# Output projection loaded in two transfers of 16 rows to a partition, last copy split over two engines, biases loaded from the ACT queue

## Chip, cores, metric

One core of one Trainium2 chip. The metric is the device time of one execution in microseconds (us), lower is better. The profiler's span (134.7 us for the kernel before) starts at the first instruction and is about 2 us shorter than the device time. Of the core's engines, PE is TensorE (matmuls), DVE is VectorE, ACT is ScalarE, Pool is GpSimd and SP is SyncE, which here only issues loads. A slice row of a profile cuts the span into 40 parts: a digit is the busy share in tenths, PEclk the clock granted to PE in tenths of full speed.

## The reference, cut to what matters

One decode step of a layer with attention and an MLP in parallel: batch 2, one token, model width 576. Attention has 32 query heads on 16 K/V heads of width 128, over the last 2048 positions of the caches.

```python
# _A_ref: q = xn @ wq; softmax over the last W = 2048 cached positions
scores = jnp.einsum("bhqd,bhkd->bhqk", q, k) * (Dh ** -0.5)
p = _softmax(scores, axis=-1)
o = jnp.einsum("bhqk,bhkd->bhqd", p, v)
return (...o.transpose(0, 2, 1, 3)...).reshape(B, Sq, Hq * Dh) @ wo     # wo: 4096 x 576
# _B_ref: relu(xn @ w1 + b1) ** 2 @ w2 + b2, w1: 576 x 4608
return x + _A_ref(xn, ...) + _B_ref(xn, ...)
```

With two rows of activations everything is a matter of reading 53.6 MB once: K and V (33.6 MB), wq, wo, w1, w2.

## The kernel before

All large loads go through SP's DMA queue, in program order. K and V come in units of four K/V heads of one batch item (eight units, 2 MB of K and 2 MB of V each). PE transposes K, ACT and DVE move K^T from PSUM to SBUF, PE forms scores, and after the softmax PE forms P·V. The results of two units (one group of 8 query heads, both batch items) go through `wo_sel`, which sorts head dimensions into the row order of the wo tile, and `wo_acc`, which multiplies by wo into the accumulator `out_ps`. The MLP's products go into the same accumulator.

```python
def issue_wo(tq):                               # WR = 8 rows of wo to a partition: 9216 contiguous bytes
    tl = wopool.tile([P, WR, D], BF16, tag="wo_sb", name=f"wo_{tq}")      # wopool: 2 buffers
    n = NC * Dh
    nc.sync.dma_start(out=tl[:], in_=A_wo[tq * n:(tq + 1) * n, :].rearrange("(p r) n -> p r n", r=WR))
# ... cut ...
def out_acc(lhsT, rhs_of, start=False, stop=False):      # two matmuls of 288 columns
    for i in range(2):
        nc.tensor.matmul(out_ps[32 * i:32 * i + B, :], lhsT=lhsT, rhs=rhs_of(i * OH, (i + 1) * OH), ...)
# ... cut: order of issue ...
load_k(1); load_v(0); load_k(2); load_v(1); issue_wo(0); load_k(3)
# ... issue_wo(1) after load_k(4); issue_wo(2), issue_wo(3) after the last V; then w2 in six pieces
for u in (NU - 2, NU - 1):
    for g in range(NG):
        pv(u, g)
wo_acc(NQ - 2)
mlp_x()                      # w2x: the rows of w2 that five small ACT-queue loads bring, 26 matmuls
wo_sel(NQ - 1)
wo_acc(NQ - 1)
for i in range(len(W2P)):    # the six w2 pieces, 68 matmuls
    mlp_o(*W2P[i], last=(i == len(W2P) - 1))
nc.vector.tensor_copy(out=fin_sb[:], in_=out_ps[:])      # 34 partitions x 288, fp32 to bf16
nc.sync.dma_start(out=out2d[:, 0:OH], in_=fin_sb[0:B, :])
nc.scalar.dma_start(out=out2d[:, OH:D], in_=fin_sb[32:32 + B, :])
```

## Time and profile before

| | before |
|---|---|
| device time, first three runs | 136.68 us (136.67 to 136.73) |
| span of the profiled run | 134.7 us |
| SP's queue | 53.32 MB in 4612 packets, 94.3% of the 16 engines' time |
| PE busy | 75% |
| last byte of w2 landed (packet records) | 131.13 us |

The third line is the one to read: a share of 16 DMA engines near its ceiling means that the time is a sum of packets. "Packet records" means the single DMA packets of the trace, with start, duration and size; the trace does not tell on which engine each ran. The lines of the views stand in the prediction.

### The profile page before, as it was taken

How to read it: one execution, taken by the hardware profiler on the slowest of the kernel's cores; microseconds unless marked ns; L12 is line 12 of the kernel's file. 1: busy time of each engine (PE TensorE's matmuls, PEld its weight loads, DVE VectorE, ACT ScalarE, POOL GpSimd, SP SyncE). 2: the span in 40 equal slices, each digit the busy share in tenths (PEclk: the TensorE clock that was granted, in tenths of full speed). 3: DMA queues.
4: the chain of work that ended last, by engine and by line, in shares of the span. 5: the costliest groups of instructions: out<-in, count | busy, mean ns of one | idle time of the engine just before them, and what ended most of it. 6: DMA issues, size and time to landing. Idle time of an engine off the chain costs nothing.

```text
span 134.7 us, 4124 instructions
## 1 busy us (share of the span) xinstructions
PE 100.8 (75%) x1876; PEld 83.2 (62%) x1876; DVE 56.9 (42%) x135; ACT 44.3 (33%) x51; POOL 9.7 (7%) x31
## 2 busy tenths in 40 slices
PE   1036797639999677998796998797194997599961
PEld 0025374639999665996786997784034997544630
DVE  7522045552277366346555655645105246500001
ACT  6706033470537207335534635421012451100000
POOL 7300000110010011001101001001100001100000
PEclk9999999555558965589996899997555579755797
DMA  4999999999999999999999999999999999999960
GB/s 152 409 422 434 428 433 419 438 414 439 404 418 439 415 412 433 410 426 429 423 428 419 423 421 422 430 415 423 408 442 428 428 424 407 416 413 424 398 235 1
DMA packets 4772, 53.87 MB, mean 400 GB/s; under 512 B 614, under 2 KB 764, under 8 KB 1280
## 3 DMA queue, kind: packets, MB, share of 16 engines
q1 hardware_dynamic: 4612, 53.32, 94.3%
q8 instruction: 14, 0.23, 0.7%
q10 hardware_dynamic: 80, 0.30, 0.5%
q0 software_dynamic: 64, 0.01, 0.0%
q14 instruction: 2, 0.02, 0.0%
HBM read 53.62 MB, written 0.00 MB: 398 GB/s over the span
## 4 chain that ended last, share of the span: by engine, by line
DMA 87%; PE 8%; SPq 2%; issue 0%; DVE 0%; ACT 0%; ACTq 0%
DMA v<-in_A_v_cache_dram 47%; DMA k<-in_A_k_cache_dram 18%; DMA w<-in_B_w_dram 16%; PE kT_ps L279 5%; DMA w2x_sb<-in_B_w_dram 5%; PE oT_ps L331 1%; PE sc_ps L294 1%; SPq L110 1%; SPq L117 1%; PE out_ps L244 1%; SPq L122 0%; DVE fin_sb L505 0%; ACT kT L282 0%; ACTq L282 0%
## 5 line engine op out<-in xcount | busy, mean ns | idle before, releaser
L279 PE MATMUL kT_ps<-ident,k 128*128 128x128 bf16 x512 | 49.5, 265 | 3.8 <-DMA k<-in_A_k_cache_dram 2.6
L279 PEld LDWEIGHTS <-k 128*128 128x128 bf16 x512 | 40.4, 121 | 5.3 <-DMA k<-in_A_k_cache_dram 2.8
L282 ACT COPY kT<-kT_ps 128x1024 bf16<-128x1024 bf16 x32 | 31.9, 1011 | 34.5 <-PE kT_ps L279 33.1
L284 DVE COPY kT<-kT_ps 128x1024 bf16<-128x1024 bf16 x32 | 21.6, 683 | 26.6 <-PE kT_ps L279 26.1
L294 PE MATMUL sc_ps<-qT_all,kT 128*128 128x8 bf16 x512 | 21.8, 168 | 5.1 <-ACT kT L282 2.6
L294 PEld LDWEIGHTS <-kT 128*128 128x128 bf16 x512 | 19.7, 101 | 7.0 <-ACT kT L282 3.4
L331 PE MATMUL oT_ps<-pT,v 128*128 128x8 bf16 x512 | 15.9, 167 | 3.9 <-DMA v<-in_A_v_cache_dram 2.2
L331 PEld LDWEIGHTS <-v 128*128 128x128 bf16 x512 | 14.5, 97 | 5.3 <-issue 2.7
L311 ACT ACTIVATE pT<-sub 128x512 bf16<-128x512 f32 x8 | 5.0, 630 | 25.8 <-DVE sub L308 25.8
L313 DVE TENSOR_REDUCE l<-pT 128x8 f32<-128x512 bf16 x8 | 8.6, 1070 | 4.7 <-ACT pT L311 4.7
L304 POOL PARTITION_ALL_REDUCE gmax<-m x8 | 2.9, 365 | 80.6 <-DVE m L302 80.6
L244 PEld LDWEIGHTS <-hT_sb 128*2 128x2 bf16 (+2 forms) x94 | 4.8, 97 | 5.1 <-issue 2.3
L300 DVE TENSOR_REDUCE m<-sc_ps 128x8 f32<-128x512 f32 x8 | 5.5, 691 | 3.8 <-PE sc_ps L294 3.5
L374 PE MATMUL h_ps<-w,xnT 128*2 128x384 bf16 x48 | 4.2, 518 | 3.2 <-DMA w<-in_B_w_dram 3.2
L244 PE MATMUL out_ps<-wo,ws 128*2 128x288 bf16 x64 | 6.5, 363 | 0.0
L244 PE MATMUL out_ps<-w,hT_sb 128*2 128x288 bf16 x68 | 5.5, 306 | 1.1 <-DMA w<-in_B_w_dram 0.8
L505 DVE CAST fin_sb<-out_ps 34x288 bf16<-34x288 f32 x1 | 0.5, 450 | 13.4 <-PE out_ps L244 13.4
L308 DVE TENSOR_TENSOR sub<-sc_ps,gm 128x512 f32<-128x512 f32 x8 | 5.5, 690 | 0.2
L374 PEld LDWEIGHTS <-xnT 128*2 128x2 bf16 x60 | 1.8, 115 | 5.8 <-issue 5.8
L315 POOL PARTITION_ALL_REDUCE lsum<-l x8 | 3.2, 398 | 24.6 <-DVE l L313 24.6
L257 PE MATMUL q_ps<-wq,xnT 128*2 128x512 bf16 x32 | 3.3, 475 | 2.0 <-DMA wq<-in_A_wq_dram 2.0
L244 PE MATMUL out_ps<-b_sb,ones_b 1*2 1x288 bf16 x2 | 0.4, 394 | 5.5 <-DMA b_sb<-in_B_b_dram 5.5
(72 smaller groups left out, 47.7 us busy)
## 6 DMA issues: line engine op xcount, KB each, us to landing
k<-in_A_k_cache_dram SPq DMA_DIRECT2D x8, 2048.0 KB, 36.0
v<-in_A_v_cache_dram SPq DMA_DIRECT2D x8, 2048.0 KB, 27.7
wo<-in_A_wo_dram SPq DMA_DIRECT2D x4, 1152.0 KB, 24.1
w<-in_B_w_dram SPq DMA_DIRECT2D x2, 2304.0 KB
wq<-in_A_wq_dram SPq DMA_DIRECT2D x2, 2048.0 KB, 14.8
w<-in_B_w_dram SPq DMA_DIRECT2D x3, 1296.0 KB
w_rem<-in_B_w_dram SPq DMA_DIRECT2D x1, 576.0 KB
w<-in_B_w_dram SPq DMA_DIRECT2D x1, 576.0 KB, 26.2
```

Of the source, the lines that this page charges most:

```text
L244: nc.tensor.matmul(out_ps[32 * i:32 * i + B, :], lhsT=lhsT, rhs=rhs_of(i * OH, (i + 1) * OH), start=start, stop=stop, skip_group_check=True)
L257: nc.tensor.matmul(q_ps[k][32 * g:32 * g + B, :], lhsT=xnT[:, xc, :], rhs=rhs, start=(c == 0), stop=(c == KC - 1), skip_group_check=True, ...
L279: nc.tensor.transpose(out=kT_ps[:, i * P:(i + 1) * P], in_=k_sb[:, j * Dh:(j + 1) * Dh], identity=ident[:])
L282: nc.scalar.copy(out=kT[:], in_=kT_ps[:])
L284: nc.vector.tensor_copy(out=kT[:], in_=kT_ps[:])
L294: nc.tensor.matmul(sc_ps[:, g * JG + i, :], lhsT=kT[:, i * P:(i + 1) * P], rhs=qT_all[:, b, tq * NC:(tq + 1) * NC], start=True, stop=True)
L300: nc.vector.tensor_reduce(out=m1[:], in_=sc_ps[:].rearrange("p j c -> p c j"), axis=AX.X, op=ALU.max)
L308: nc.vector.tensor_tensor(out=sub[:], in0=sc_ps[:], in1=gm2[:].unsqueeze(1).to_broadcast([P, NJ, NC]), op=ALU.subtract)
L311: nc.scalar.activation(out=pT[:], in_=sub[:], func=ACT.Exp, scale=scale)
L313: nc.vector.tensor_reduce(out=l1[:], in_=pT[:].rearrange("p j c -> p c j"), axis=AX.X, op=ALU.add)
L331: nc.tensor.matmul(oT_ps[:], lhsT=v_sb[:, j * Dh:(j + 1) * Dh], rhs=pT_tiles[u][:, j, :], start=(j == 0), stop=(j == NJ - 1))
L374: nc.tensor.matmul(mlp["ps"][k][32 * g:32 * g + B, :], lhsT=xnT[:, xc, :], rhs=rhs, start=False, stop=(c == KC - 1), skip_group_check=True ...
```

## The change

Its intent: fewer, larger wo packets and half as many projections, each of twice the matmuls; a shorter last copy; less work on Pool.

```diff
-    WR = NC * Dh // P
+    WR = 2 * NC * Dh // P                    # 16 rows to a partition: 18432 bytes
-    wopool = ctx.enter_context(tc.tile_pool(name="wopool", bufs=2))
+    wopool = ctx.enter_context(tc.tile_pool(name="wopool", bufs=1))
+        n = P * WR                           # in issue_wo: two loads of 2304 KB
 ... selection matrix: one memset and one reduction in place of eight copies on Pool (cut) ...
 ... wo_sel: two head groups at once, 16 selection matmuls (cut) ...
-    issue_wo(0) ... issue_wo(1) ... issue_wo(2) ... issue_wo(3)
+        if u == 4:
+            issue_wo(0)                      # before w1
+    issue_wo(1)                              # before w2
-    nc.gpsimd.dma_start(out=b1_sb[:], ...)   # and b2
+    nc.scalar.dma_start(out=b1_sb[:], ...)
     step(NU - 1, {}, with_pv=False)
+    for g in range(NG):
+        pv(NU - 2, g)
+    mlp_x()                                  # its matmuls kept in program order
+    for g in range(NG):
+        pv(NU - 1, g)
+    wo_sel(1)
+    wo_acc(1)
-    nc.vector.tensor_copy(out=fin_sb[:], in_=out_ps[:])
+    nc.vector.tensor_copy(out=fin_sb[:, 0:half_o], in_=out_ps[:, 0:half_o])
+    nc.scalar.copy(out=fin_sb[:, half_o:OH], in_=out_ps[:, half_o:OH])
```

More of the change, by code (lines that the diff above doesn't have):

```diff
@@ L79 @@
     OH = D // 2
-    WR = NC * Dh // P
+    NP = NQ // 2
+    WR = 2 * NC * Dh // P
     DW = Dh // WR
@@ L136, in w_rows, with issue_wo @@
         return tiles[c][:, col0 - sg * L:col0 - sg * L + n], NFULL + sg
-    def issue_wo(tq):
-        tl = wopool.tile([P, WR, D], BF16, tag="wo_sb", name=f"wo_{tq}")
-        n = NC * Dh
-        nc.sync.dma_start(out=tl[:], in_=A_wo[tq * n:(tq + 1) * n, :].rearrange("(p r) n -> p r n", r=WR))
-        wo_tiles[tq] = tl
+    def issue_wo(t):
+        tl = wopool.tile([P, WR, D], BF16, tag="wo_sb", name=f"wo_{t}")
+        n = P * WR
+        nc.sync.dma_start(out=tl[:], in_=A_wo[t * n:(t + 1) * n, :].rearrange("(p r) n -> p r n", r=WR))
+        wo_tiles[t] = tl
     w2_last = []
@@ L229 @@
     rmask = const.tile([P, WR], BF16, name="rmask")
-    gsel = const.tile([P, DW], BF16, name="gsel")
-    sel = const.tile([P, NC, NC, DW], BF16, name="sel")
+    MZ = (2 * NC - 1) * DW
+    sel = const.tile([P, 2 * MZ + DW], BF16, name="sel")
     nc.gpsimd.memset(sel[:], 0.0)
@@ L234, with out_acc @@
         nc.vector.tensor_reduce(out=rmask[:], in_=ident[:].rearrange("p (c r) -> p r c", r=WR), axis=AX.X, op=ALU.add)
-        nc.vector.tensor_reduce(out=gsel[:], in_=ident[:].rearrange("p (c r) -> p c r", r=WR), axis=AX.X, op=ALU.add)
-    for h in range(NC):
-        nc.gpsimd.tensor_copy(out=sel[:, h, h, :], in_=gsel[:])
+        nc.vector.tensor_reduce(out=sel[:, MZ:MZ + DW], in_=ident[:].rearrange("p (c r) -> p c r", r=WR), axis=AX.X,
+                                op=ALU.add)
     out_ps = psum.tile([32 + B, OH], F32, tag="out", name="out_ps")
     nc.vector.memset(out_ps[:], 0.0)
-    def out_acc(lhsT, rhs_of, start=False, stop=False):
+    def out_acc(lhsT, rhs_of, start=False, stop=False, pin=False):
         for i in range(2):
-            nc.tensor.matmul(out_ps[32 * i:32 * i + B, :], lhsT=lhsT, rhs=rhs_of(i * OH, (i + 1) * OH),
-                             start=start, stop=stop, skip_group_check=True)
+            mm = nc.tensor.matmul(out_ps[32 * i:32 * i + B, :], lhsT=lhsT, rhs=rhs_of(i * OH, (i + 1) * OH),
+                                  start=start, stop=stop, skip_group_check=True)
+            if pin:
+                tc.keep_in_program_order(mm)
     qT_all = const.tile([P, B, Hq], BF16, name="qT_all")
@@ L339, with wo_sel @@
     wo_state = {}
-    def wo_sel(tq):
-        oG = oG_tiles.pop(tq)
-        rr = work.tile([P, WR, NC * B], BF16, tag="rr", name=f"rr_{tq}")
-        nc.vector.tensor_tensor(
-            out=rr[:],
-            in0=oG[:].rearrange("p h b -> p (h b)").unsqueeze(1).to_broadcast([P, WR, NC * B]),
-            in1=rmask[:].unsqueeze(2).to_broadcast([P, WR, NC * B]), op=ALU.mult)
-        wps = psum.tile([P, WR, B], F32, tag="misc", bufs=2, name=f"wps_{tq}")
-        for h in range(NC):
-            nc.tensor.matmul(wps[:], lhsT=sel[:, h, :, :].rearrange("p a c -> p (a c)"),
-                             rhs=rr[:, :, h * B:(h + 1) * B], start=(h == 0), stop=(h == NC - 1))
-        ws = work.tile([P, WR, B], BF16, tag="ws", name=f"ws_{tq}")
+    def wo_sel(t):
+        rr = work.tile([P, WR, 2 * NC * B], BF16, tag="rr", bufs=1, name=f"rr_{t}")
+        for i in range(2):
+            oG = oG_tiles.pop(2 * t + i)
+            nc.vector.tensor_tensor(
+                out=rr[:, :, i * NC * B:(i + 1) * NC * B],
+                in0=oG[:].rearrange("p h b -> p (h b)").unsqueeze(1).to_broadcast([P, WR, NC * B]),
+                in1=rmask[:].unsqueeze(2).to_broadcast([P, WR, NC * B]), op=ALU.mult)
+        wps = psum.tile([P, WR, B], F32, tag="misc", bufs=2, name=f"wps_{t}")
+        for h in range(2 * NC):
+            nc.tensor.matmul(wps[:], lhsT=sel[:, MZ - h * DW:MZ - h * DW + P],
+                             rhs=rr[:, :, h * B:(h + 1) * B], start=(h == 0), stop=(h == 2 * NC - 1))
+        ws = work.tile([P, WR, B], BF16, tag="ws", name=f"ws_{t}")
         nc.vector.tensor_copy(out=ws[:], in_=wps[:])
-        wo_state[tq] = ws
+        wo_state[t] = ws
     def wo_acc(tq):
@@ L410, in mlp_x @@
             w = w2x_sb[0:m, i * D:(i + 1) * D] if m == XP else w2y_sb[:]
-            out_acc(mlp["h"][0:m, N3 + FT + i, :], lambda a, z: w[:, a:z])
+            out_acc(mlp["h"][0:m, N3 + FT + i, :], lambda a, z: w[:, a:z], pin=True)
     def load_k(u):
@@ L430 @@
     load_v(1)
-    issue_wo(0)
     load_k(3)
@@ L454 @@
     b1_sb = const.tile([NG4, HW], BF16, name="b1_sb")
-    nc.gpsimd.dma_start(out=b1_sb[:], in_=B_b1.rearrange("(g n) -> g n", g=NG4))
+    nc.scalar.dma_start(out=b1_sb[:], in_=B_b1.rearrange("(g n) -> g n", g=NG4))
     sel4 = const.tile([NG4, P], BF16, name="sel4")
@@ L459 @@
     b2_sb = const.tile([1, D], BF16, name="b2_sb")
-    nc.gpsimd.dma_start(out=b2_sb[:], in_=B_b2.rearrange("(o n) -> o n", o=1))
+    nc.scalar.dma_start(out=b2_sb[:], in_=B_b2.rearrange("(o n) -> o n", o=1))
     step(1, {})
     load_k(4)
-    issue_wo(1)
     out_acc(ident[:B, :B], lambda a, z: x_sb[:, a:z], start=True)
@@ L466 @@
     for u in range(2, NU - 1):
-        hooks = {}
-        if u >= 4 and u % B == 0:
-            hooks = {3: [lambda t=u // B - 2: wo_sel(t)], 6: [lambda t=u // B - 2: wo_acc(t)]}
-        step(u, hooks)
+        step(u, {})
         if u + 1 < NU - 1:
@@ L479 @@
             load_v(NU - 1)
-            issue_wo(2)
-    issue_wo(3)
+    issue_wo(1)
     for w in W2P:
@@ L486 @@
         pv(NU - 3, g)
-    mlp_h_block(0)
-    mlp_h_block(1)
-    wo_sel(NQ - 2)
-    for c in range(2, KC):
+    wo_sel(0)
+    wo_acc(0)
+    for c in range(KC):
         mlp_h_block(c)
@@ L493 @@
     step(NU - 1, {}, with_pv=False)
-    for u in (NU - 2, NU - 1):
-        for g in range(NG):
-            pv(u, g)
-    wo_acc(NQ - 2)
+    for g in range(NG):
+        pv(NU - 2, g)
     mlp_x()
-    wo_sel(NQ - 1)
-    wo_acc(NQ - 1)
+    for g in range(NG):
+        pv(NU - 1, g)
+    wo_sel(1)
+    wo_acc(1)
     for i in range(len(W2P)):
@@ L504 @@
     fin_sb = work.tile([32 + B, OH], BF16, tag="fin", name="fin_sb")
-    nc.vector.tensor_copy(out=fin_sb[:], in_=out_ps[:])
+    half_o = OH // 2
+    nc.vector.tensor_copy(out=fin_sb[:, 0:half_o], in_=out_ps[:, 0:half_o])
+    nc.scalar.copy(out=fin_sb[:, half_o:OH], in_=out_ps[:, half_o:OH])
     nc.sync.dma_start(out=out2d[:, 0:OH], in_=fin_sb[0:B, :])
```

## The prediction

> **What bounds the kernel now.** I began with the slice table of the page, which says whether one resource is full all the way.
>
> ```profile
> PE   1036797639999677998796998797194997599961
> ...
> PEclk9999999555558965589996899997555579755797
> DMA  4999999999999999999999999999999999999960
> GB/s 152 409 422 434 428 433 419 438 414 439 404 418 439 415 412 433 410 426 429 423 428 419 423 421 422 430 415 423 408 442 428 428 424 407 416 413 424 398 235 1
> ```
>
> The DMA row stands at nine tenths or more from the second slice to the thirty-eighth, at 400 to 440 GB/s, while PE has holes. The chain of waits agrees, and its last pieces show the tail.
>
> ```profile
> DMA 87%; PE 8%; SPq 2%; issue 0%; DVE 0%; ACT 0%; ACTq 0%
> ```
> ```profile
> 109.10 22.13 DMA w<-in_B_w_dram
> 131.23 0.04 issue
> 131.27 0.68 PE out_ps L244 x6
> 131.97 0.45 DVE fin_sb L505
> ```
>
> The last piece of w2 lands, six matmuls follow it, one DVE copy of 0.45 us empties the accumulator, and the output leaves: 3.5 us of 134.7 after the last byte. In the packet records behind these views, 16 packets are in flight on average in each us from 3 us to 127 us, one for each DMA engine, and never fewer than 14. Then comes a ragged end: some engines finish at 127.5 us, and about seven go on to 130.9 to 131.1 us. Most of this kernel is thus a fixed sum of packets. It gets faster only if a packet costs less or the 3.5 us tail gets shorter; it gets slower if the queue ever runs dry.
>
> How far is it from dry? I set each load's issue on SP against its first packet.
>
> ```profile
> 19.05 0.33 SPq L141 DMA_DIRECT2D wo<-in_A_wo_dram  x1
> 20.30 0.54 SPq L110 DMA_DIRECT2D k<-in_A_k_cache_dram  x1
> 30.43 0.54 SPq L110 DMA_DIRECT2D v<-in_A_v_cache_dram  x1
> 37.07 0.53 SPq L110 DMA_DIRECT2D k<-in_A_k_cache_dram  x1
> 37.66 0.58 SPq L141 DMA_DIRECT2D wo<-in_A_wo_dram  x1
> ```
>
> The first wo, issued at 19.05, has its first 9216-byte packet at 37.89; the second, issued at 37.66, at 55.5. The K load between them, issued at 37.07, starts at 51.7: the smallest lead of the K and V loads that the reorder touches is 14 us. SP waits much (for PE to free K buffers, for old transfers), but always for a load that is needed 14 to 29 us later.
>
> **What the Trainium skill says.** "DMA: Bandwidth & Descriptors", section "Why small descriptors are slow (HBM only)", says that a packet carries a fixed overhead whatever its length. The packet records agree: a 9216-byte packet took 351 ns (median; mean 355.3, 512 of them, all wo), an 18432-byte one 689 ns (mean 694.5, 256, all w1). Two of the one cost 13 ns (means: 16 ns) more than one of the other, 2%: at these sizes little is left to gain. The same page, on how many engines a DMA uses (section "Why a DMA increments its semaphore by 16 and not by 1"), says a transfer of n partitions runs on the largest divisor up to 16, on the lowest-numbered engines from SP or ACT. The trace has five 13824-byte packets for each five-partition w2x load, as that says; which engines they ran on it does not record. "PSUM — Partial Sum Buffer", section "PSUM bank collisions raise a hardware error", says two engines must not touch one bank and quadrant of 32 partitions at once, reads against reads included, and that schedulers put a dependency between them. The trace before has nothing of it (one engine reads the accumulator), but the changed program as built has: see the last copy. "TensorE: Matmul & The Clock Gate", section "Part 1: The HAM clock gate", says the clock is halved or full by activity in windows of about 3.4 us; the clock records here switch between 1.0 and 0.5 in stretches of 3.4, 6.8, 10.2 and so on, which agrees.
>
> **The change part by part.**
>
> *wo in two transfers.* The bytes are equal: 4 x 1152 KB become 2 x 2304 KB. Packets go from 512 of 9216 bytes to 256 of 18432, so each of 16 engines does 16 in place of 32: 32 x 355.3 = 11.37 us against 16 x 694.5 = 11.11 us, a gain of 0.26 us (0.21 by medians). Two transfers fewer also save each engine two 4-byte semaphore packets of 9 ns, 0.02 us. The stream is full, so this 0.28 us does come off its end.
>
> *The order of loads.* In the program's order the first two wo loads, 2.8 us of stream each, leave the early K/V stretch; the merged one comes after the last V load before w1, the second before w2. K and V thus arrive up to 5.6 us earlier in the middle, and buffers must be free 5.6 us earlier. Leads of 14 us and more become about 8 to 10 us: no gap. The rotation of the eight transfer semaphores shifts as well (the second K load now waits for the first to land, 7.8 us, where it had been issued at 3.1), but its first packet is due only at 18.3. The second wo uses the first one's buffer and waits for its 32 matmuls, which stand after V unit 5, about 92 to 95 us; it is due at about 110. So no wait here reaches the end: 0.
>
> *Biases from the ACT queue.* The Pool queue's packets go (64, of which 44 are 4-byte ones; 0.06 us per engine in sum), and b1 is still four packets of about 93 ns. b2 becomes one packet of about 51 ns in place of sixteen of 12 ns. If those fall on the engines that end last, they give back up to 0.06 us; say 0.03. A side effect is in the middle: the build places b2's two matmuls after sixteen of the q projection, and ACT issues the load only after its third K^T copy, about 18.7 us; earlier ACT loads needed 3.3 to 4 us from issue to first packet. PE may wait some 3 us near 20 us. It then falls into later holes (PE waited 2.17 us for V at 30.4), and is not on the stream's path: 0.
>
> *Selection matrix on Pool.* Eight copies of 192 ns and most of a 951 ns memset go, at 0.7 to 6 us, beside the first load: 0.
>
> *PE's order.* The counts are equal (32 selection and 64 wo matmuls), but the first two wo groups leave the middle, and the w2x block is fixed between the last two PV blocks.
>
> ```profile
> 115.49 1.81 PE L331 MATMUL oT_ps<-pT,v 128*128 128x8 bf16 x64 [1.50 <-ACT pT L311]
> ...
> 123.51 2.08 PE L244 MATMUL out_ps<-wo,ws 128*2 128x288 bf16 x16
> 125.38 2.91 PE L244 MATMUL out_ps<-w,hT_sb 128*2 128x288 bf16 x36
> 129.11 2.83 PE L244 MATMUL out_ps<-w,hT_sb 128*2 128x288 bf16 x32 [0.81 <-DMA w<-in_B_w_dram]
> ```
>
> PE now stands 1.50 us before the last PV, waiting for the softmax. The w2x block (3.2 us at 120.3) fills this, so the last PV starts about 117.2 and ends 119.0. Mask and selection (16 matmuls, twice 0.36) with their copies take to about 120.8; 32 wo matmuls, twice 2.08 us, to about 125.0, against 125.38 now. PE then waits for the third w2 piece at 129.1 as it does now, with the slack 0.81 grown to about 1.2. A gain where PE isn't awaited: 0.
>
> *The last copy.* Meant to halve 0.45 us. But the built program shows ACT's half waiting for DVE's last instruction, that is, for the other half: both read one bank in the same quadrants. Both output transfers then wait for ACT. DVE's half: from 172 ns for 16 columns (the ws copy) and 450 for 288, about 1.02 ns a column, so about 302 ns for 144. ACT's half: 587 ns for 512 columns (the q copy) and 1011 for 1024, 0.83 ns a column, so about 282 ns. A hand-over from DVE to ACT took 40 ns in the softmax (a subtraction ending at 114.77, the exponential at 114.81). Together 302 + 40 + 282 = 624 ns: 0.17 us more than now, on the path.
>
> Sum: -0.28 + 0.03 + 0.17 = -0.08 us, so 136.6 us. The shorter stream and the longer copy nearly cancel.
>
> **The rivals.** (1) The halves overlap after all: max(302, 282) in place of 450 saves 0.15, and the time would be 136.3. Against it stands the wait in the build; for it only the intent. (2) A dry queue: if PE, delayed at 20 us by b2 or late with K^T copies, frees buffers more than 8 us late, the queue would stand still for the excess, and each us lost would be a us at the end: 138 to 140. For it: PE is at seven to nine tenths in most slices after the fifth, and wo was ballast that let it catch up. Against it: the leads above, and PE's holes waiting for K and V (2.17, 1.02, 0.57 us), which say it is fed by the stream and not the other way round. (3) The clock at the end. PE's w2 matmuls ran at full clock from 126.5 us; at half they cost 130 ns each (2.08 us for 16) in place of about 66 to 80. If the changed order leaves PE at half clock there, the 32 after 129.1 us take about 4.2 us in place of 2.86, and the time becomes about 137.9. Against it: the wo and w2 matmuls stand back to back in the window before 126.5, as they do now. (4) The stream gains more, because the ragged end changes: were the engines that end last relieved by another placement of small packets, up to 1 us lies there, but the change leaves the w2x loads as they are.
>
> **Range and chances.** The sum rests on two small terms with an uncertainty of about 0.1 us each; rival 1 pulls to 136.3, rivals 2 and 3 to 137 and over with perhaps one chance in ten together. Hence 136.6 with 136.2 to 137.0. Over 2% is 2.7 us: faster would need three quarters of the 3.5 us tail, 1 in 100; slower needs a dry queue, 2 in 100; within 2%, 97 in 100.
>
> **What would show it.** wo packets of about 690 ns, 256 of them; the DMA row still full; the last w2 piece landing about 0.25 us earlier (next to the last copy's start, 131.97 now, 131.7 then); the last copy as a DVE piece of about 0.30 and then, not beside it, an ACT piece of about 0.28 that waited for DVE. I am wrong if a slice of the DMA row drops in the middle, if the two halves stand beside each other, if PE reaches the third w2 piece after it has landed, or if the 18432-byte packets of wo are slower than those of w1.

## The result and the profile after

| | before | changed |
|---|---|---|
| median of 6 runs | 136.68 us (136.39 to 136.73) | 136.22 us (136.06 to 136.71) |
| span of the profiled run | 134.67 us | 134.42 us |
| last byte of w2 landed | 131.13 us | 130.84 us |
| last copy, start to end | 0.45 us | 0.61 us |
| output landed | 133.30 us | 133.14 us |

The ratio is 0.9976, 95% interval 0.9958 to 0.9993: 0.24% faster. (Ratios here are the mean time of one kernel's fast runs over that of the other's fast runs in the same rounds, so not quite the ratio of the medians quoted. A run counts as slow when it is over 1.5% above the fastest of its kernel; one is, the 139.95 of "filled, half packets".)

The slice rows of the changed kernel, to set beside those of before:

```profile
PEclk9999779777799757999869869856855599555999
DMA  4999999999999999999999999999999999999950
GB/s 147 400 445 406 451 410 434 419 444 421 423 424 424 399 429 414 439 410 439 414 439 402 449 416 433 433 411 422 402 447 424 434 417 428 416 415 406 411 232 1
```

The DMA row is as full as before. The end of its chain of waits (start us, us, what):

```profile
104.03 26.93 DMA w<-in_B_w_dram
130.96 0.04 issue
131.00 0.64 PE out_ps L244 x6
131.64 0.02 issue
131.66 0.31 DVE fin_sb L503
131.97 0.02 issue
132.00 0.27 ACT fin_sb L504
```

Everything up to the copy is 0.31 us earlier than before (131.66 against 131.97), and the copy gives back 0.16: 0.31 on DVE, then 0.27 on ACT, one after the other.

The middle, from the timeline of PE. Where the changed kernel waits for b2:

```profile
21.81 0.28 PE L244 MATMUL out_ps<-b_sb,ones_b 1*2 1x288 bf16 x2 [1.41 <-DMA b_sb<-in_B_b_dram]
```

And its tail:

```profile
115.24 1.82 PE L333 MATMUL oT_ps<-pT,v 128*128 128x8 bf16 x62
...
119.35 4.00 PE L244 MATMUL out_ps<-wo,ws 128*2 128x288 bf16 x32 [0.56 <-DMA wo<-in_A_wo_dram]
...
123.14 1.73 PE L244 MATMUL out_ps<-w,hT_sb 128*2 128x288 bf16 x18
...
125.66 1.27 PE L244 MATMUL out_ps<-w,hT_sb 128*2 128x288 bf16 x18 [0.79 <-DMA w<-in_B_w_dram]
...
128.82 2.80 PE L244 MATMUL out_ps<-w,hT_sb 128*2 128x288 bf16 x32 [1.89 <-DMA w<-in_B_w_dram]
```

The last PV is no longer preceded by an idle wait. PE runs ahead of w2: it waits 0.79 us for the second piece and 1.89 us for the third, where before it waited 0.81 us for the third alone. That surplus of idle time returns below. PE also waits 0.56 us for the second wo tile, which is now one load and lands whole, its last packet at 118.83 us.

### The profile page after: what moved, and what is told of

Its sections match the earlier page's. It is cut to its first block, busy times and chain, and to the rows that moved or that the text cites. A ratio compares the mean times of both kernels' runs of the same rounds, so it can differ in the third digit from the quotient of the medians.

```text
span 134.4 us, 4107 instructions
## 1 busy us (share of the span) xinstructions
PE 98.5 (73%) x1876; PEld 81.9 (61%) x1876; DVE 56.5 (42%) x133; ACT 44.4 (33%) x52; POOL 6.7 (5%) x21
## 4 chain that ended last, share of the span: by engine, by line
DMA 77%; PE 12%; DVE 4%; ACT 2%; issue 1%; POOL 1%; SPq 0%; ACTq 0%
DMA k<-in_A_k_cache_dram 44%; DMA w<-in_B_w_dram 20%; DMA wq<-in_A_wq_dram 9%; PE kT_ps L281 5%; DMA b_sb<-in_B_b_dram 3%; PE oT_ps L333 2%; PE sc_ps L296 2%; ACT kT L284 2%; PE q_ps L259 1%; DVE m L302 1%; DVE sub L310 1%; PE out_ps L244 1%; POOL gmax L306 1%; DVE qrow L264 1%; SPq L111 0%
## 5 line engine op out<-in xcount | busy, mean ns | idle before, releaser
L281 PE MATMUL kT_ps<-ident,k 128*128 128x128 bf16 x512 | 47.4, 258 | 2.9 <-DMA k<-in_A_k_cache_dram 1.5
L281 PEld LDWEIGHTS <-k 128*128 128x128 bf16 x512 | 39.1, 118 | 4.0 <-DMA k<-in_A_k_cache_dram 1.7
L296 PEld LDWEIGHTS <-kT 128*128 128x128 bf16 x512 | 18.9, 99 | 9.2 <-ACT kT L284 4.3
L333 PE MATMUL oT_ps<-pT,v 128*128 128x8 bf16 x512 | 15.4, 167 | 2.1 <-ACT kT L284 1.7
L244 PE MATMUL out_ps<-wo,ws 128*2 128x288 bf16 x64 | 8.0, 442 | 1.2 <-DVE ws L356 0.7
L244 PEld LDWEIGHTS <-ws 128*2 128x2 bf16 x64 | 3.9, 121 | 4.4 <-DVE ws L356 1.2
L387 DVE TENSOR_TENSOR hrow<-t 98x384 bf16<-98x384 f32 x3 | 1.6, 556 | 9.7 <-ACT t L386 9.6
```

The source lines that it names most:

```text
L244: mm = nc.tensor.matmul(out_ps[32 * i:32 * i + B, :], lhsT=lhsT, rhs=rhs_of(i * OH, (i + 1) * OH), start=start, stop=stop, skip_group_chec ...
L281: nc.tensor.transpose(out=kT_ps[:, i * P:(i + 1) * P], in_=k_sb[:, j * Dh:(j + 1) * Dh], identity=ident[:])
L296: nc.tensor.matmul(sc_ps[:, g * JG + i, :], lhsT=kT[:, i * P:(i + 1) * P], rhs=qT_all[:, b, tq * NC:(tq + 1) * NC], start=True, stop=True)
L333: nc.tensor.matmul(oT_ps[:], lhsT=v_sb[:, j * Dh:(j + 1) * Dh], rhs=pT_tiles[u][:, j, :], start=(j == 0), stop=(j == NJ - 1))
```

## The experiments

Twelve experiments on eleven programs, all correct, and all "same" as before by the 2% rule. "Landing" is the end of the last w2 packet in the profiled run. The first four ran on one chip and shared its runs of the kernel before, then the next four, then the last four. The kernel before averaged 136.62 us in the rounds of the result and 136.53, 136.51 and 136.49 on the three chips, so times from different chips are not to be set side by side to better than about 0.1 us.

| run | median us (lowest to highest) | ratio to before, 95% | landing | output landed |
|---|---|---|---|---|
| one copy | 136.07 (135.95 to 137.03) | 0.9981 (0.9960 to 1.0003) | 130.73 | 132.87 |
| split only | 136.72 (136.65 to 136.84) | 1.0016 (1.0003 to 1.0029) | 131.23 | 133.56 |
| wo only | 136.29 (136.13 to 136.86) | 0.9987 (0.9972 to 1.0002) | 130.82 | 132.96 |
| half packets | 136.64 (136.24 to 137.54) | 1.0018 (0.9990 to 1.0045) | 131.15 | 134.27 |
| filled wait | 135.97 (135.89 to 136.09) | 0.9962 (0.9950 to 0.9973) | 130.68 | 132.82 |
| even engines | 138.38 (137.61 to 138.57) | 1.0124 (1.0100 to 1.0147) | 132.17 | 134.28 |
| small packets | 137.44 (137.31 to 137.58) | 1.0069 (1.0057 to 1.0082) | 131.75 | 134.37 |
| biases only | 136.61 (136.55 to 136.73) | 1.0010 (0.9997 to 1.0022) | 131.28 | 133.43 |
| filled, split | 136.19 (136.09 to 136.27) | 0.9978 (0.9966 to 0.9990) | 130.91 | 133.20 |
| filled, half packets | 137.54 (136.38 to 139.95) | 1.0070 (1.0028 to 1.0112) | 130.94 | 133.10 |
| four K/V buffers | 137.46 (137.14 to 137.83) | 1.0072 (1.0056 to 1.0089) | 132.01 | 134.16 |
| filled wait, again | 136.09 (135.95 to 136.12) | 0.9968 (0.9956 to 0.9980) | 130.93 | 133.06 |

The two runs of one program ("filled wait" and "again") landed at 130.68 and 130.93: a single landing is good to about a quarter of a us, no better.

Several programs have one group of close times and a few longer ones. I call the longer ones late and the rest undisturbed. That division was made after the times were seen; all but the 139.95 are fast runs by the rule, and the ratios in the table contain them.

### One copy

The changed kernel with the old last copy.

```diff
-    nc.vector.tensor_copy(out=fin_sb[:, 0:half_o], in_=out_ps[:, 0:half_o])
-    nc.scalar.copy(out=fin_sb[:, half_o:OH], in_=out_ps[:, half_o:OH])
+    nc.vector.tensor_copy(out=fin_sb[:], in_=out_ps[:])
```

> The changed kernel with the last copy back in one DVE instruction. Theory A (the two halves of the copy stand one after the other on the path, so the split costs time): the copy takes 0.45 us again in place of 0.30 + 0.04 + 0.27 = 0.61, and the kernel is 0.16 us faster than the changed one, about 0.45 us (0.3 per cent) faster than before; the last w2 piece lands at about 130.8 us as in the changed kernel. Rival (the split helps or does nothing): the same as the changed kernel or slower, up to 0.15 us.

Measured: 136.07 us, with four of six runs at 135.95 to 136.08 and two late ones at 136.50 and 137.03. The four lie mostly below the changed kernel's typical 136.06 to 136.23, as theory A has it, but the two were timed in different rounds, between which the kernel before differs by 0.09 us, and the late runs spoil the interval. The cost of the split rests on the next run and on the filled pair further down. The late runs needed an explanation of their own.

### Split only

The kernel before with the split copy: the same edit the other way round.

> The kernel before with only the last copy split over DVE and ACT. Theory A: 0.16 us slower than before (0.1 per cent), the last w2 piece landing unchanged at about 131.1 us, a DVE piece of 0.30 us and then an ACT piece of 0.27 us that waits for it. Rival (the halves can overlap, the split is the gain): 0.15 us faster.

Measured: ratio 1.0016, 0.2 us slower, the interval clear of 1. The end of its chain of waits:

```profile
131.37 0.69 PE out_ps L244 x6
132.06 0.02 issue
132.08 0.31 DVE fin_sb L506
132.39 0.02 issue
132.41 0.27 ACT fin_sb L507
```

ACT starts when DVE has ended, in this kernel too. The split copy is a loss of itself.

### wo only

The changed kernel with one copy and the biases back on Pool.

```diff
-    nc.scalar.dma_start(out=b1_sb[:], ...)
+    nc.gpsimd.dma_start(out=b1_sb[:], ...)     # b2 likewise
```

> The changed kernel with one copy and with the biases back on the Pool queue, so wo alone is changed (its packets, its place in the order, its matmuls). Theory A (the merged wo packets shorten the stream by 0.28 us and the biases give nothing): the last w2 piece lands at 130.8 to 130.9 us, and the time is within 0.1 us of the kernel with one copy. Rival B (the biases on the ACT queue brought the gain, by taking the small packets of the Pool queue out of the stream or by another clock): the last piece lands at 131.0 to 131.1 us, as before.

Measured: landing 130.82, as in the changed kernel (130.84), five runs at 136.13 to 136.40 and one late at 136.86. The median is 0.22 us above "one copy", more than the 0.1 I had allowed; with late runs in both, I don't read a gain of the biases from it. It is a warning, though: without the late runs the difference is still 0.22 us, while the landings differ by 0.09, so differences of this size between undisturbed runs (0.30 and 0.37 below) are loose.

### Biases only

The kernel before with the two bias loads on the ACT queue.

> The kernel before with the two bias loads on the ACT queue, nothing else. Theory A: the stream ends as before within 0.1 us (131.1 us), the time is within 0.1 us of before; PE may stand some 3 us near 20 us for b2, which does not reach the end. Rival B: the stream ends 0.2 to 0.3 us earlier.

Measured: ratio 1.0010, landing 131.28. No gain. PE waited 1.0 us for b2 at 22 us, and nothing of it reached the end.

### Half packets

"One copy" with each 16-row tile loaded by two transfers: the new order and the new matmuls, but the old packets.

```diff
-        nc.sync.dma_start(out=tl[:], in_=A_wo[t * n:(t + 1) * n, :].rearrange("(p r) n -> p r n", r=WR))
+        rows = A_wo[t * n:(t + 1) * n, :].rearrange("(p r) n -> p r n", r=WR)
+        for i in range(2):
+            h = WR // 2
+            nc.sync.dma_start(out=tl[:, i * h:(i + 1) * h, :], in_=rows[:, i * h:(i + 1) * h, :])
```

> The changed kernel with one copy, where each merged wo tile is loaded by two DMAs of 8 rows to a partition in place of one of 16: 512 packets of 9216 bytes again, in the new order and with the new matmuls. Theory A (packet overhead): each engine has 32 packets of 355 ns in place of 16 of 693, and two more semaphore packets, so the last w2 piece lands 0.28 us later than in the kernel with one copy, at 131.1 us. Rival C (the order of loads or of the matmuls brought the gain): it still lands at 130.8 us.

Measured: landing 131.15, 0.42 us later than in "one copy", which speaks for theory A and against C. But half of its runs were late, the profiled one (137.54) among them, so its profile shows what a late run is. The timeline of PE, then the stretch of 129 to 132 us of this kernel (columns: stretch, length, busy us and instructions of PE, PEld, DVE, ACT and POOL, granted clock, DMA share, GB/s):

```profile
125.97 1.27 PE L247 MATMUL out_ps<-w,hT_sb 128*2 128x288 bf16 x18 [1.75 <-DMA w<-in_B_w_dram]
...
129.11 3.80 PE L247 MATMUL out_ps<-w,hT_sb 128*2 128x288 bf16 x32 [1.88 <-DMA w<-in_B_w_dram]
```
```profile
129.00:132.00 3.00, 2.89 (x26) 1.66 (x27) 0.00 (x0) 0.00 (x0) 0.00 (x0) 0.53 0.36 139
```

The same stretch of "one copy", whose profiled run was a good one:

```profile
129.00:132.00 3.00, 2.24 (x30) 1.15 (x26) 0.45 (x1) 0.00 (x0) 0.00 (x0) 1.00 0.28 107
```

The same 32 matmuls took 3.80 us in place of 2.80, because the granted clock was 0.53 in place of 1.00. Its clock record falls at 129.18 us, at the end of a stretch of 3.4 us in which PE had done little but those 18 matmuls (it was busy for 1.34 us of it). In "one copy" the same steps of 3.4 us end at 127.65 and 131.07, so that its idle time lies in two of them (PE busy for 1.93 and 2.10 us) and the clock stays up: where the steps lie differs from run to run. So the copy begins at 132.95, 1.0 us late, with the bytes on time. This was rival 3 of the prediction, and it did happen in this run. No other late run has a profile, so that they all come from the clock is not shown.

### Filled wait

If the idle wait before the third w2 piece makes the clock fall, real work put there should end the late runs: "one copy", with the w2x matmuls moved from before the last PV block to behind the second w2 piece.

```diff
-    mlp_x()                     # between the last two PV blocks
     for i in range(len(W2P)):
+        if i == 2:
+            mlp_x()
         mlp_o(*W2P[i], last=(i == len(W2P) - 1))      # these matmuls now kept in program order as well
```

> The changed kernel with one copy, and with the w2x matmuls moved from before the last PV block to between the second and the third w2 piece, where PE waited 1.89 us for the third piece. Theory D (the new order leaves PE idle there so long that in some runs the clock falls to half in the last 3 us, which makes runs of 136.5 to 137.5 us among those of 136.0): no run over 136.4 us, all within about 0.3 us of each other, median about 136.0; the matmuls after the third piece at full clock, 2.8 us. Rival E (the late runs come from something else, say the stream): as many late runs as the kernel with one copy, about 2 of 6. The last w2 piece should land as in that kernel, at 130.7 to 130.9 us; PE reaches the third piece at about 128.7 us, just as it lands.

Measured: five runs at 135.89 to 136.09, ratio 0.9962. PE now:

```profile
126.69 1.63 PE L244 MATMUL out_ps<-w2x_sb,hT_sb 20*2 20x288 bf16 x24
128.16 0.29 PE L244 MATMUL out_ps<-w2y_sb,hT_sb 16*2 16x288 bf16 x2
128.65 2.81 PE L244 MATMUL out_ps<-w,hT_sb 128*2 128x288 bf16 x32 [0.20 <-DMA w<-in_B_w_dram]
```

The wait of 1.89 us is 0.20, and no run is late, as theory D has it. This is the lowest time, and its interval lies under that of the kernel before; beside the changed kernel it was not run, and the two intervals against before overlap.

### Filled wait again, and filled with the split copy

The same program once more, and the changed kernel whole (split copy) with the wait filled.

> The kernel with one copy and the filled wait, again, as the base of the two above on the same chip: 135.9 to 136.1 us, no late run, the third w2 piece's matmuls at full clock.

> The changed kernel, split copy and all, with the w2x matmuls moved into the wait for the third w2 piece. The cost of the split where no late run disturbs it. Theory A: 0.16 us slower than the same with one copy (run again beside it), so about 136.1 us, and no run over 136.4 us. Rival: equal to it within 0.05 us or faster.

Measured on one chip: 136.09 (135.95 to 136.12) and 136.19 (136.09 to 136.27); the means of the five runs are 136.05 and 136.19, so the split costs 0.14 us here and 0.2 in the kernel before. Its profile has 0.30 and 0.27 us one after the other. Of the kernels with two wo transfers, the 15 runs with a filled wait have no time over 136.27; the 18 without (changed, one copy, wo only) have four over 136.45 (136.50, 136.71, 136.86, 137.03). That speaks for theory D but does not prove it: so uneven a split comes by chance about once in 13 times, and the filled kernels did not run beside unfilled ones on one chip.

### Filled with half packets

> The kernel with one copy and the filled wait, with wo in four DMAs of 9216-byte packets. The cost of the packets where no late run disturbs it. Theory A: 0.28 us slower than the same with two DMAs, so about 136.25 us; the last w2 piece lands 0.28 us later than its. Theory D: no run over 136.6 us, where the unfilled one had 136.85, 137.22 and 137.54. Rival C (order alone): equal within 0.1 us.

Measured: the two undisturbed runs are 136.38 and 136.46, 0.37 us above the mean of the filled kernel, near the 0.28 of theory A; without the filling, the three undisturbed runs of "half packets" (136.24, 136.33, 136.43) stood 0.30 above the four of "one copy". Landing, though, was 130.94, equal to the comparison's, not 0.28 later; given the quarter of a us from profile to profile, I trust the times. And theory D's part failed here: four runs were late, at 136.96, 138.13, 138.24 and 139.95, although the wait was filled. None of these was the profiled one. What makes them late is open. The one profile, of an undisturbed run, has the wait filled and the clock up (0.21 us of wait, 2.81 us for the 32 matmuls); of the late runs nothing is recorded but their times. So filling the wait does not end late runs as such, and part of those of "half packets" may have this other cause.

### Small packets

"One copy" with wo in sixteen transfers of two rows to a partition.

```diff
+        for a in range(0, WR, 2):            # written here as one loop
+            nc.sync.dma_start(out=tl[:, a:a + 2, :], in_=rows[:, a:a + 2, :])
```

> The changed kernel with one copy, and each wo tile loaded by eight DMAs of two rows to a partition: 2048 packets of 2304 bytes, 128 for each engine, in place of 16 of 18432. The packet cost by itself, enlarged. Theory A: 128 x 94.5 ns less 16 x 693.5 ns is 1.0 us, and 14 more transfers with a 9 ns semaphore packet are 0.13 us, so the last w2 piece lands 1.1 us later than in the kernel with one copy, at 131.9 us, and the time is 137.2 us. Rival (the packet overhead hides behind the other engines or the memory): it lands within 0.3 us of 130.8 us.

Measured: landing 131.75, 1.02 us later than "one copy" (0.8 to 1.1 later than the six profiles with 18432-byte wo packets), and 137.44 us, 1.4 above "one copy". The rival is out: the cost of packets reaches the end. The clock fell at 131.15 in its profiled run and took 0.4 us more for the last 32 matmuls (3.24 against 2.80). It is a second case of what "half packets" showed: in the 3.4 us before the fall PE was busy for 1.36 us.

### Four K/V buffers

```diff
-    kvpool = ctx.enter_context(tc.tile_pool(name="kvpool", bufs=6))
+    kvpool = ctx.enter_context(tc.tile_pool(name="kvpool", bufs=4))
```

> The changed kernel with one copy and four K and V buffers in place of six, which takes about two loads (10 us) of the lead that the queue has. My step (the leads of 12 us and more are slack): the smallest leads fall to about 2 to 7 us, no slice of the DMA row drops, the time stays within 0.3 us of the kernel with one copy. Rival 2 (the queue is near dry): slices of the DMA row fall under nine tenths in the middle and the time grows by 1 us or more.

Measured: 137.46 us, landing 132.01. My step failed at this dose: the fourth K load was issued at 37.5 us and had a lead of 1.1 us from the end of its issue, and the stream thinned for a moment. Its GB/s row:

```profile
GB/s 141 402 456 422 429 426 426 426 426 424 419 339 402 408 433 406 440 406 440 426 416 433 411 440 424 430 419 430 393 450 421 431 423 437 407 406 418 409 214 1
```

One slice at 339, from 37.2 to 40.6 us (its digit in the DMA row is 8), and 1.1 to 1.3 us lost at the end, of which about 1.0 was lost by the next V load. Elsewhere leads of 3.6 to 7 us kept the row full. So rival 2 is the right picture of how this kernel would get slow; the change is just not near it.

### Even engines

The end of the stream is ragged, and five engines carry the w2x loads. "One copy" with the last 256 rows of w2 as one transfer to 32 partitions, which all 16 engines share.

```diff
-    XR, XP, XE = 12, 20, 5
+    XR, XP, XE = 8, 32, 32          # and no 16-row remainder
```

> The changed kernel with one copy, and the last 256 rows of w2 as one load of 32 partitions of 9216 bytes, which all 16 DMA engines share, in place of four loads of five partitions of 13824 bytes and one of 16. Theory F (the end of the stream is ragged because five engines carry 2.07 us that the others don't, on top of the instruction fetches): each engine carries 0.7 us of it, the last w2 piece lands 0.4 to 0.9 us earlier, at 129.9 to 130.4 us, the time is about 135.5. Rival G (the fetches alone, or other things, make the same engines late): the last piece lands at 130.6 us or later, nothing gained.

Measured: 138.38 us, slower by 1.2%; landing 132.17. Neither theory. Its GB/s row:

```profile
GB/s 155 391 386 360 420 423 421 439 410 454 391 449 410 434 417 425 429 420 434 420 425 429 410 453 431 417 407 434 405 432 429 420 438 422 406 424 423 406 163 1
```

That landing is of a run of 137.62 us; another took 137.61, the other four 138.35 to 138.57, and of those there is no profile. While that transfer was in flight (8 to 10.5 us) the stream fell to 295 and 262 GB/s (the stretches 9 to 10 and 10 to 11 us), and K and wq packets of 16384 bytes that began between 8 and 10 us took 995 ns in the mean where "one copy" had 618. The Trainium skill, "SBUF — State Buffer", section "Door 1: The DMA port swizzle", has it that partitions 0 to 31 reach only eight of the 16 DMA ports; sixteen engines pushing into them together is consistent with what the packets show, though no run here counts ports. A rival is as open: two queues now take turns on all sixteen engines, and a 16384-byte packet of 613 ns and a 9216-byte one of 347 ns together are 960 ns. The lag behind "one copy", averaged over the 128 packets of each load, was 1.6 us at the second K load and came down to 1.0 us by the sixth V load, since "one copy" has half of its w2x bytes still to load. Less this 1.0 us the landing would be about 131.2, no earlier than that of "one copy": an estimate from these two numbers, nearer to rival G. For the end stayed ragged: each of the 14 instruction fetches (16384 bytes, about 1.07 us, one every 6 to 15 us) sets one engine back by about 1.5 us when packets are chained end to start (a gap of about 1.05 us in the loads, then one packet about 0.5 us longer), and the engines were spread over 3.2 us at the end with the w2x bytes even. A layout that evens the engines without crowding the same partitions was not run.

## Why the prediction was right

The prediction was 136.6 (136.2 to 137.0), the result 136.22, 0.02 us inside the lower end of the range. There is luck in that: the measured change, -0.33 us, is four times the -0.08 of the sum, and 136.22 is nearer to the 136.3 of rival 1, which the trace rules out, than to 136.6. What holds up is the mechanism. By its steps:

- **The stream bounds the kernel.** Right. The DMA row is full in both, and changes of packets ("small packets") or of supply ("four K/V buffers", "even engines") move the landing and the time together.
- **wo in two transfers, -0.28 us.** The mechanism is right, the size about right. The records of the changed kernel have 18432-byte packets of 693.5 ns in the mean, so 32 x 355.3 less 16 x 693.5 is 0.27 us an engine, as worked out. But kernels with two wo transfers landed at 130.82 in the mean (six profiles), those with the old loads at 131.21 (three): 0.39. The two with the old packets in the new order (131.15 and 130.94) landed 0.23 later than the six. Undoing the merge alone gave 0.30 and 0.37 in undisturbed times. These lie around 0.28; what is above it is within the spread of landings and stays unexplained.
- **Biases, +0.03 and no gain.** Right: nothing moved at the end. PE waited 1.4 us for b2, not 3: ACT issued its load earlier than I took from the order (at 17.1 us, not 18.7).
- **The order of loads, 0.** Right. The smallest lead among the moved loads was 12 us (predicted 8 to 10), issued here and first seen at 49.0:

```profile
36.38 0.54 SPq L111 DMA_DIRECT2D k<-in_A_k_cache_dram  x1
```

- **The last copy, +0.17 us.** Right, in mechanism and size: 0.30 + 0.04 + 0.27 against 0.45. In times it was 0.14 to 0.2. The dependency was legible in the built program, and rival 1 (overlap) is out. Which way it went was decided by the program as built; what the halves would do without the dependency was not run.
- **PE's order, 0.** Half right, and the weakest step. The w2x block filled the softmax wait as worked out, but PE got further ahead than I had it: the clock was full from 124.1 us, not 126.5, and the wait before the third piece became 1.89 us, not 1.2. The wait of 0.56 us for the merged wo tile was not foreseen at all, and cost nothing. I wrote that nobody waits for PE there. True of the good runs; but a long wait can cost PE its clock for the last 32 matmuls, as the profiles of "half packets" and "small packets" show. The change has late runs that the kernel before does not have (one of 6; of the kernel before, 39 runs, none over 136.78); that the clock made them is the likely cause, not a shown one.
- **Sum.** -0.08 predicted; -0.33 by the ratio. In the two profiles the stream moved by -0.29 and the copy by +0.16, so the output landed 0.16 us earlier: close to the sum. The rest of the -0.33 is not located. The averages over profiles would put it in the stream (about -0.4 in place of -0.25), within the spread of landings.

So the kernel got faster by its packets, gave 0.15 us of it back through the split copy, and, it seems, traded a little steadiness for idle time in the wrong place. With the split undone and the wait filled it runs at 135.97 to 136.09 us, 0.3 to 0.4% under before, without late runs in ten.

## What to carry to other kernels

When the DMA row is full from end to end, work out the packets: count times duration from the records gave 0.28 us here, and the landings moved by 0.2 to 0.4. As long as the queue stays fed, what other engines do counted only after the last byte, as the copy and the clock did here. Before splitting a copy over two engines, look whether both halves read one PSUM bank; if they do, look whether the built program puts them in series; here it did, and the split was a loss. And where PE must wait for the last bytes, leave it real work to do in that wait, since idle time just before the tail can halve the clock in it, as two profiles here show.

## What the Trainium skill lacked or had wrong

- "DMA: Bandwidth & Descriptors", section "Why small descriptors are slow (HBM only)", gives the fixed cost of a packet as about three cycles and has joining descriptors as worth it only up to 256 bytes. Here it is about 10 ns a packet up to 18 KB (medians 95, 179, 349 and 688 ns for 2304, 4608, 9216 and 18432 bytes: twice one less the next is 11, 9 and 10 ns), and it reached the end of a full stream.
- "Runtime: NRT & Kernel Launch", section "Instruction fetch mechanics", has the fetches as DMA in blocks of 16 KiB, which the trace shows, but not what they cost a full stream of loads: 14 packets of 16384 bytes and about 1.07 us in each run, each setting one engine back by about 1.5 us, so that engines ended 3.2 us apart even when the loads were even.
- "SBUF — State Buffer", section "Door 1: The DMA port swizzle", gives the bandwidth of a transfer to few partitions by itself. The section lacks what others in flight lose meanwhile: 16384-byte packets took 995 ns in place of 618 beside a load to 32 partitions. No run here separates the ports from the two queues' taking turns.
- "PSUM — Partial Sum Buffer", section "PSUM bank collisions raise a hardware error", says that a scheduler puts a dependency between two such readers; the build had it, and the traces show the halves in series. What the enforced order costs is not there: a hand-over of 0.04 us and a second fixed cost, 0.61 us for two halves against 0.45 for the whole.
- "TensorE: Matmul & The Clock Gate", section "Part 1: The HAM clock gate", describes the windows. For modelling, it puts the penalty of the clock's ramp at less than 1% of a typical span; here a fall of the clock cost that little, 1.0 us of 136, yet three times the whole gain of the change. The two falls in question came though no wait of PE was longer than 1.91 us.
